# A Fourier filter with a maxout layer on one core: the first transform on bf16 loads without a fold, and another order for the exchanges

## The chip, the cores and the metric

The kernel runs on one core of a Trainium2 chip. TensorE (PE) multiplies matrices, VectorE (DVE) and ScalarE (ACT) move results out of PSUM and do elementwise work, GpSimd (POOL) does elementwise work and issues DMAs, SyncE (SP) issues DMAs. All DMAs of the core share its 16 DMA engines. The metric is the device time of one execution in microseconds, lower is better.

## What is computed

```python
def _attn_ref(x, filt_r, filt_i):            # x: 8 x 3072 x 256, filters: 1537 x 256
    X = np.fft.rfft(x, axis=1)
    F = (filt_r + 1j * filt_i)[None, :, :]
    Y = X * F
    return np.fft.irfft(Y, n=x.shape[1], axis=1).astype(np.float32)

def _moe_ref(x, w1, w2, w_out):              # x: 24576 x 256, w1, w2: 256 x 1024, w_out: 1024 x 256
    h1 = x @ w1
    h2 = x @ w2
    g = np.maximum(h1, h2)
    return (g @ w_out).astype(np.float32)
```

Each of the eight sequences is filtered in the frequency domain along its 3072 points, and each of the 24576 results goes through a layer with two sets of weights, of whose products the larger is taken. All inputs and the output are float32.

## The kernel before

**The transform.** 3072 points are 128 x 24. A batch of x is 128 partitions (p) by 24 columns (n) by 256 channels (d). S1 (`f1`, line 434) is a 128-point transform over p, one matmul for each two columns. Its result goes out to a DRAM buffer `ad` and comes back as `bt` in another arrangement (`f1_read`, 453): the 24 columns now lie on partitions, 48 rows in each half. Then `s2` (72) transforms over n into `px`, `product` (82) multiplies with the filter `F` on DVE, and `s3` (468) transforms back with the tables VP and VQ into `zt`. `zt` goes out to DRAM (`zd`) and comes back as `zr` (`z_read`, 460, three DMAs). `s4` (501) is the last 128-point transform, into `yt`: 512 tokens a tile, six tiles a batch. These two round trips through DRAM are the exchanges. A bt read moves 1.5 MB in four DMAs of runs of 512 bytes, a zr read 1.5 MB in three.

**The layer.** max(h1, h2) is h2 + max(h1 - h2, 0). `moe_h` (516) multiplies with Wd = w1 - w2, one of eight column blocks j at a time, into `ph`, and ACT or DVE takes max(., 0) into `gt`. `moe_o` (532) multiplies `gt` with Wo and `yt` with M = w2 Wo, and every tile ends in one `out` DMA of 512 KB, issued by POOL.

**S1 in the before kernel** works on folded input. `load_x` (419) brings fp32 rows with two DMAs of 512 KB, `fold` (427) on POOL makes sum and difference of two halves in bf16, and `f1` does four matmuls of 64 x 64 into two PSUM tiles, one of which ACT and one of which DVE evicts. Six `f1` a batch; every second one writes 512 KB to `ad`.

**Batch 0** goes without DRAM: `load_x0` (115) loads bf16 (POOL's DMA casts), `f1t` (254), `t1` (292), `s3t` (306) and `t2` (327) transpose on PE instead. Tables of sines come from ACT (`table_c`, 162, and lines 217 to 220 for U). The filter is loaded by POOL's DMAs in four pieces of rows (`load_f`, 125), each copied to the odd rows by SP (`double_f`, 136); its unused rows 48 to 63 are filled with zeros by DMAs from a small tile (`zero_f`, 140). The weights w1 and w2 share a buffer with `bt` and so are loaded late (line 378).

**The order.** The whole order is written out by hand. Tile tt of the layer has eight steps 8 tt + j; each step does `moe_h` of tile tt, `moe_o` of tile tt - 1, and then what the plan has put there; `s4` of the next tile follows at j = 4, or j = 6 where a new batch begins (its first tile is transformed in step 48 b - 2). `plan_batch` (560) takes, for a batch b, the steps of its loads, folds, `f1`, of the bt read, of the nine halves of the transform (s2 of one group and s3 of the group before), and of the zr read. Engines and queues take their work in this order, but each runs as far ahead as its own waits allow: SP's queue holds the ad writes, zd writes, bt and zr reads; POOL's holds the x loads, the folds and the outs. For batches from 4 on, with o = 48 (b - 2), the before plan has loads at o - 20, o - 8 and o, folds at o + 2, o + 6, o + 10, `f1` from o + 8 in steps of 3, the bt read at o + 28, s2 and s3 from o + 48 in steps of 4, and the zr read at o + 84. Batches 1 to 3 have lines of their own.

Of the kernel before, what the change touches and what calls it, by code (L numbers as in the profile page):

```python
# [21 lines left out]
TWO_PI = 6.283184  # L22
# [4 lines left out]
def kernel(  # L27
# [11 lines left out]
    nc = tc.nc  # L39
    V, S, G, TE = nc.vector, nc.scalar, nc.gpsimd, nc.tensor  # L40
# [4 lines left out]
    CF = const.tile([128, 128], BF16)  # L45
# [15 lines left out]
    xpool = ctx.enter_context(tc.tile_pool(name="xpool", bufs=3))  # L61
    sdpool = ctx.enter_context(tc.tile_pool(name="sdpool", bufs=2))
    apool = ctx.enter_context(tc.tile_pool(name="apool", bufs=2))
# [4 lines left out]
    bt = {}  # L68
# [36 lines left out]
    zf = tb.tile([16, 1024], BF16)  # L105
# [9 lines left out]
    def load_x0(c):  # L115
        if c % 3 == 0:
            xb["t"] = gpool.tile([128, 3, 4, D], BF16, tag="gt", name="xb")
        t_ = xb["t"][:, c % 3]
        G.dma_start(out=t_, in_=x[0].rearrange("(p n) d -> p n d", n=N2)[:, 4 * c:4 * c + 4, :])
        xb[c] = t_  # L120
# [15 lines left out]
    def double_f(s0, s1):  # L136
        for h in range(2):
            nc.sync.dma_start(out=F[64 * h + 1:64 * h + 48:2, :, s0:s1], in_=F[64 * h:64 * h + 48:2, :, s0:s1])

    def zero_f(s0, s1):  # L140
        for ri in range(2):
            n = (s1 - s0) // 4
            nc.sync.dma_start(out=F[48:64, ri, s0:s1].rearrange("p (k t) d -> p k (t d)", t=4),
                              in_=zf.rearrange("p (o d) -> p o d", o=1).to_broadcast([16, n, 1024]))
# [11 lines left out]
    uc = tb.tile([128, 2, 2, 64], FP32)  # L156
    rc = tb.tile([128, 2, 2, 64], FP32)
    col = tb.tile([128, 16], FP32)
    bb, mm, aa, n2, pp, pf, nn2 = (col[:, i:i + 1] for i in range(7))


    def table_c(k, p):
        V.tensor_scalar(uc[:, k, 0], row[:, 0:64], p, 0.25, OP.mult, OP.add)
        V.tensor_scalar(uc[:, k, 1], row[:, 0:64], p, None, OP.mult)
        V.tensor_scalar(uc[:, k, 1, 0:1], p, 64.0, 0.25, OP.mult, OP.add)
        wrap(uc[:, k], rc[:, k])
        if k == 0:
            S.activation(CE, uc[:, k].rearrange("p a x -> p (a x)"), AF.Sin, bias=zero, scale=TWO_PI)
        for r in range(2):
            S.activation((CF if k else C1)[:, 64 * r:64 * r + 64].rearrange("p (t a) -> p t a", a=2),  # L170
                         uc[:, k].rearrange("p a (t r) -> p r t a", r=2)[:, r], AF.Sin, bias=zero, scale=TWO_PI)
# [199 lines left out]
    for g in range(8):  # L371
        if g + 1 < 8:
            px[g + 1] = s2(0, g + 1, pxp, "px")
            products(g + 1)
        if g + 3 < 8:
            t1(g + 3, S)
        s3t(g, pq.pop(g), (S, S) if g < 7 else (S, V))
        if g == 4:
            wt = bpool.tile([128, 2, 2, HID], FP32, tag="bt", name="wt")
            w1f, w2f = wt[:, 0], wt[:, 1]  # L380
            for k in range(2):
                for w_, f_ in ((w2f, moe_w2), (w1f, moe_w1)):
                    nc.sync.dma_start(out=w_[:, :, 512 * k:512 * k + 512],
                                      in_=f_.rearrange("(c p) j -> p c j", p=128)[:, :, 512 * k:512 * k + 512])
# [28 lines left out]
    ad = {}  # L413
    zd = {}
    x2 = {}
    sd = {}
    at_ = {}

    def load_x(b, c):
        t_ = xpool.tile([128, 2, 4, D], FP32, tag="x2", name="x2")  # L420
        for h in range(2):
            src = bass.AP(x.tensor, x.offset + (b * N + 12 * h + 4 * c) * D,
                          [[N2 * D, 64], [64 * N2 * D, 2], [1, 4 * D]])
            G.dma_start(out=t_[64 * h:64 * h + 64].rearrange("p k n d -> p k (n d)"), in_=src)
        x2[b, c] = t_

    def fold(b, c):
        t_ = sdpool.tile([128, 2, 4, D], BF16, tag="sd", name="sd")
        x_ = x2.pop((b, c))
        G.tensor_tensor(t_[:, 0], x_[:, 0], x_[:, 1], OP.add)  # L430
        G.tensor_tensor(t_[:, 1], x_[:, 0], x_[:, 1], OP.subtract)  # L431
        sd[b, c] = t_

    def f1(b, n):
        c, u = divmod(n, 2)
        if n == 0:
# [4 lines left out]
        pa = [ps.tile([128, 2, D], FP32, tag="ps", name="pa") for _ in range(2)]
        for a in range(2):
            for h in range(2):
                TE.matmul(pa[h][64 * a:64 * a + 64], CF[64 * h:64 * h + 64, 64 * a:64 * a + 64],  # L444
                          sd[b, c][64 * h:64 * h + 64, a, 2 * u:2 * u + 2], start=True, stop=True,
                          skip_group_check=True)
        S.activation(at[:, 0, 2 * u:2 * u + 2], pa[0], AF.Copy)  # L447
        V.tensor_copy(at[:, 1, 2 * u:2 * u + 2], pa[1])  # L448
        if u == 1:
            nc.sync.dma_start(out=ad[b].rearrange("r (h n) d -> r h (n d)", h=2)[:, :, 4 * c * D:4 * c * D + 4 * D],  # L450
                              in_=at.rearrange("p h n d -> p h (n d)"))
# [186 lines left out]
```

## Time and profile before

| | before |
|---|---|
| median of 3 runs | 626.75 us (626.73 to 627.84) |
| the profiled execution, its own time | 625.69 us |
| its span, first to last instruction | 623.9 us |
| PE busy | 519.4 us (83%) |
| DVE, ACT, POOL busy | 323.2, 331.4, 186.5 us |
| mean granted TensorE clock | 0.913 |
| moved by DMA | 99.89 MB, 160 GB/s |
| x loads | 42 of 512 KB |
| first `ph` matmul (the layer begins) | 54.9 us |
| step 47, 95, 143, 191, 239 (first `gt` after a new batch's first tile) | 163.9, 237.7, 307.0, 376.4, 445.2 us |

Instructions are grouped by the line of the kernel; `out<-in` names tiles. "PE py L507 <- DMA zr<-zd: 41.7, 5, 11.1" says that PE's instruction of line 507 waited 41.7 us in total, five times, at most 11.1, for that DMA. In the chain of waits each row has a start, a length and what filled it. An `SPq` row in the timeline shows SP issuing DMAs; a DMA's data moves later.

### The profile page before, as it was taken

To read this page: it belongs to the slowest core of one execution; us is meant where nothing else is said; L and a number is where in the kernel's file an instruction comes from. 1 tells how busy PE (TensorE), PEld (TensorE's weight loads), DVE (VectorE), ACT (ScalarE), POOL (GpSimd) and SP (SyncE) were. 2 spreads that over 40 slices of the span, in tenths; PEclk is the share of its full clock that TensorE was granted. 3 is DMA by queue.
4 is the path that set the end of the run, shared out by engine and by line. 5 is a ranking of instruction groups with operands and counts; after the bars stand their busy time and mean duration, and the time that the engine had idled before them with its cause. 6 is when DMAs were issued, how large, how long until landed. Compare 5 with 4: busy or idle time off the path is not lost.

```text
span 623.9 us, 12287 instructions
## 1 busy us (share of the span) xinstructions
PE 519.4 (83%) x5094; PEld 349.0 (56%) x5172; DVE 323.2 (52%) x434; ACT 331.4 (53%) x587; POOL 186.5 (30%) x186
## 2 busy tenths in 40 slices
PE   5566580897699938999499959999699999999996
PEld 3344360564466625667366636667366666667774
DVE  6656330693158705773277515873277447733332
ACT  5462250465257624766266635765366656665551
POOL 6666851232343016411181017311370000000000
PEclk9856795799699988999799988999799999999999
DMA  7957799139976996469853994569844952351112
GB/s 124 147 129 174 172 257 147 51 95 255 275 104 202 195 178 203 138 173 201 239 156 101 232 253 134 153 166 233 227 128 134 174 208 81 99 187 76 59 45 101
DMA packets 73641, 99.89 MB, mean 160 GB/s; under 512 B 5809, under 2 KB 51378, under 8 KB 73586
## 3 DMA queue, kind: packets, MB, share of 16 engines
q1 hardware_dynamic: 55874, 48.25, 36.2%
q0 software_dynamic: 17712, 50.87, 30.7%
q8 instruction: 40, 0.66, 0.5%
q14 instruction: 15, 0.12, 0.1%
HBM read 53.48 MB, written 47.19 MB: 161 GB/s over the span
## 4 chain that ended last, share of the span: by engine, by line
PE 51%; DMA 21%; issue 17%; POOL 5%; DVE 2%; ACT 2%; SPq 1%; POOLq 0%; DVEq 0%; ACTq 0%
PE po L542 18%; PE ph L522 17%; DMA zr<-zd 6%; DMA zd<-zt 5%; PE pz L478 4%; PE po L545 4%; PE py L507 3%; DMA bt<-ad 3%; DMA F<-in_filt_r_dram 2%; PE pa L444 2%; PE px L78 2%; DMA ad<-at 2%; DVE pqt L85 2%; DMA xb<-in_x_dram 1%; DMA x<-in_x_dram 1%
## 5 line engine op out<-in xcount | busy, mean ns | idle before, releaser
L527 ACT ACTIVATE gt<-ph 128x512 bf16<-128x512 f32 x334 | 199.2, 597 | 134.7 <-PE ph L522 130.3
L542 PE MATMUL po<-Wo,gt 128*128 128x256 bf16 x1536 | 234.2, 276 | 4.4 <-issue 1.1
L522 PE MATMUL ph<-yt,Wd 128*128 128x512 bf16 x691 | 218.5, 389 | 4.0 <-DVE Wd L388 2.0
L542 PEld LDWEIGHTS <-gt 128*128 128x128 bf16 x1536 | 152.5, 99 | 102.5 <-issue 6.6
L85 DVE TENSOR_TENSOR pqt<-px,F 112x1024 bf16<-112x1024 f32 x124 | 146.0, 1219 | 80.0 <-PE px L78 71.7
L551 POOL DMA_DIRECT2D out_dram<-ot x48 | 26.8, 559 | 377.0 <-DVE ot L547 364.6
L547 DVE COPY ot<-po 128x512 f32<-128x512 f32 x96 | 66.1, 689 | 116.4 <-PE po L545 116.1
L522 PEld LDWEIGHTS <-Wd 128*128 128x128 bf16 x768 | 69.6, 100 | 27.8 <-issue 18.1
L482 ACT ACTIVATE zt<-pz 112x512 bf16<-112x512 f32 x112 | 60.7, 594 | 33.6 <-PE pz L478 32.0
L545 PE MATMUL po<-M,yt 128*128 128x256 bf16 x384 | 74.8, 277 | 0.0
L507 PE MATMUL py<-G,zr 128*128 128x128 bf16 x384 | 33.4, 234 | 43.2 <-DMA zr<-zd 41.7
L511 DVE TENSOR_SCALAR yt<-py 128x512 bf16<-128x512 f32 x48 | 32.9, 685 | 63.8 <-PE py L507 63.8
L509 ACT ACTIVATE yt<-py 128x512 bf16<-128x512 f32 x48 | 28.7, 599 | 67.5 <-PE py L507 67.4
L430 POOL TENSOR_TENSOR sd<-x 128x1024 bf16<-128x1024 f32 x21 | 49.4, 2353 | 37.3 <-issue 32.4
L507 PEld LDWEIGHTS <-zr 128*128 128x128 bf16 x384 | 25.9, 105 | 51.1 <-DMA zr<-zd 43.1
L431 POOL TENSOR_TENSOR sd<-x 128x1024 bf16<-128x1024 f32 x21 | 49.3, 2348 | 0.0
L78 PE MATMUL px<-bt,U 48*64 48x256 bf16 x512 | 27.9, 287 | 17.1 <-DMA bt<-ad 17.1
L545 PEld LDWEIGHTS <-yt 128*128 128x128 bf16 x384 | 38.2, 100 | 5.0
L525 DVE TENSOR_SCALAR gt<-ph 128x512 bf16<-128x512 f32 x50 | 34.1, 682 | 7.9 <-PE ph L522 7.8
L447 ACT ACTIVATE at<-pa 128x512 bf16<-128x512 f32 x42 | 25.1, 598 | 22.9 <-PE pa L444 22.5
L448 DVE CAST at<-pa 128x512 bf16<-128x512 f32 x42 | 28.6, 682 | 14.4 <-PE pa L444 11.0
L478 PE MATMUL pz<-pqt,VP 48*64 48x256 bf16 x448 | 30.7, 283 | 0.6 <-DVE pqt L85 0.2
(119 smaller groups left out, 280.1 us busy)
## 6 DMA issues: line engine op xcount, KB each, us to landing
out_dram<-ot POOLq DMA_DIRECT2D x48, 512.0 KB, 3.2
x<-in_x_dram POOLq DMA_DIRECT2D x42, 512.0 KB, 8.9
ad<-at SPq DMA_DIRECT2D x21, 512.0 KB, 4.2
bt<-ad SPq DMA_DIRECT2D x28, 384.0 KB, 13.0
zd<-zt SPq DMA_DIRECT2D x112, 96.0 KB, 3.0
zr<-zd SPq DMA_DIRECT2D x7, 768.0 KB, 8.4
zr<-zd SPq DMA_DIRECT2D x7, 512.0 KB, 6.6
wt<-in_moe_w_dram SPq DMA_DIRECT2D x4, 512.0 KB, 4.2
```

What stands on the lines that cost most here:

```text
L78: TE.matmul(px[r][64 * h:64 * h + 64, i], U[64 * r:64 * r + 48, 48 * t:48 * t + 64], bt[b][64 * r:64 * r + 48, t], start=True, stop=True, ...
L85: E.tensor_tensor(pqt, px[0:112].rearrange("p (o i) d -> p o i d", o=1).to_broadcast([112, 2, 2, D]), F[0:112, :, s0:s0 + 3:2], OP.mult)
L430: G.tensor_tensor(t_[:, 0], x_[:, 0], x_[:, 1], OP.add)
L431: G.tensor_tensor(t_[:, 1], x_[:, 0], x_[:, 1], OP.subtract)
L478: TE.matmul(pz[h][64 * r:64 * r + 64, i], W_[64 * h:64 * h + 48, c0_:c0_ + 64], pq[r][64 * h:64 * h + 48, ri, i], start=(ri == 0), stop=(r ...
L482: S.activation(zt[:, h, 2 * (g % 2):2 * (g % 2) + 2], pz[h][0:112], AF.Copy)
L507: TE.matmul(py[:, n], zr[b][:, 4 * i + n, 128 * dc:128 * dc + 128], G1, start=True, stop=True)
L522: TE.matmul(ph_, Wd[:, dc, 128 * j:128 * j + 128], y_[:, dc].rearrange("p a b -> p (a b)"), start=(dc == 0), stop=(dc == 1))
L527: S.activation(gt[tt][:, j], ph_, AF.Relu)
L542: TE.matmul(p_, g_[:, jj, 128 * n:128 * n + 128], Wo[:, jj], start=(jj == 0), stop=False)
L545: TE.matmul(p_, y_[:, dc, n], M[:, dc], start=False, stop=(dc == 1))
L547: V.tensor_copy(ot[tt][:, n - 1:n + 1], po[tt])
```

## The change

S1 takes the input as it is: `load_x` is one DMA that casts to bf16 (512 KB read, 256 KB written, all 128 partitions), `f1` is one matmul of 128 x 128 by 512 columns with the table C1 and one eviction, by ACT or DVE in turn, and every second of the now twelve `f1` a batch writes 256 KB to `ad`. The folds, their buffers and the table CF are gone. The plan has new steps for loads, `f1`, bt reads, transforms and zr reads. Batch 0's input comes in four pieces, of 8, 8, 4 and 4 columns. The filter comes in three pieces, and its zero rows are written by DVE, POOL and ACT, as part of a 32-row block that the loads then write into. U's sines come after three `f1t`, the table SW after those. The weights have a buffer of their own and are loaded behind the filter.

```diff
-    xpool = ctx.enter_context(tc.tile_pool(name="xpool", bufs=3))
-    sdpool = ctx.enter_context(tc.tile_pool(name="sdpool", bufs=2))
-    apool = ctx.enter_context(tc.tile_pool(name="apool", bufs=2))
+    xpool = ctx.enter_context(tc.tile_pool(name="xpool", bufs=8))
+    apool = ctx.enter_context(tc.tile_pool(name="apool", bufs=6))
+    wpool = ctx.enter_context(tc.tile_pool(name="wpool", bufs=1))
...
-    def load_x0(c):
-        if c % 3 == 0:
-            xb["t"] = gpool.tile([128, 3, 4, D], BF16, tag="gt", name="xb")
-        t_ = xb["t"][:, c % 3]
-        G.dma_start(out=t_, in_=x[0].rearrange("(p n) d -> p n d", n=N2)[:, 4 * c:4 * c + 4, :])
-        xb[c] = t_
+    for n0, n1 in ((0, 8), (8, 16), (16, 20), (20, 24)):
+        if n0 % 16 == 0:
+            xt = gpool.tile([128, 16, D], BF16, tag="gt", name="xt")
+        G.dma_start(out=xt[:, n0 % 16:n0 % 16 + n1 - n0], in_=x[0].rearrange("(p n) d -> p n d", n=N2)[:, n0:n1, :])
+        for n in range(n0, n1, 4):
+            xb[n // 4] = xt[:, n % 16:n % 16 + 4]
...
     def zero_f(s0, s1):
-        for ri in range(2):
-            n = (s1 - s0) // 4
-            nc.sync.dma_start(out=F[48:64, ri, s0:s1].rearrange("p (k t) d -> p k (t d)", t=4),
-                              in_=zf.rearrange("p (o d) -> p o d", o=1).to_broadcast([16, n, 1024]))
+        return F[32:64, :, s0:s1].rearrange("p c s d -> p c (s d)")
...
     V.memset(hpi, 1.570796)
+    V.memset(zero_f(0, 8), 0.0)
+    G.memset(zero_f(8, 20), 0.0)
+    for ri in range(2):
+        S.activation(F[32:64, ri, 20:32].rearrange("p s d -> p (s d)").bitcast(FP32), zero[32:64].to_broadcast([32, 1536]), AF.Copy)
...
-    S.activation(Uq[:, :, 0], v.rearrange("p t s j -> p t (s j)"), AF.Sin, bias=zero, scale=TWO_PI)
...
+    def table_u():
+        S.activation(Uq[:, :, 0], v.rearrange("p t s j -> p t (s j)"), AF.Sin, bias=zero, scale=TWO_PI)
+        S.activation(Uq[:, :, 1], rv.rearrange("p t s j -> p t (s j)"), AF.Sin, bias=hpi, scale=-TWO_PI)
...
-    for c in range(6):
-        load_x0(c)
-    load_f(0, 8)
-    double_f(0, 8)
-    zero_f(0, 8)
-    zero_f(8, 32)
-    for s0, s1 in ((8, 20), (20, 28), (28, 32)):
+    for s0, s1 in ((0, 8), (8, 20), (20, 32)):
         load_f(s0, s1)
         double_f(s0, s1)
+    wt = wpool.tile([128, 2, 2, HID], FP32, name="wt")
+    w1f, w2f = wt[:, 0], wt[:, 1]
+    for k in range(2):
+        for w_, f_ in ((w2f, moe_w2), (w1f, moe_w1)):
+            nc.sync.dma_start(out=w_[:, :, 512 * k:512 * k + 512],
+                              in_=f_.rearrange("(c p) j -> p c j", p=128)[:, :, 512 * k:512 * k + 512])
...
+    def load_x(b, c):
+        t_ = xpool.tile([128, 4, D], BF16, tag="xb", name="xb")
+        G.dma_start(out=t_, in_=x[b].rearrange("(p n) d -> p n d", n=N2)[:, 4 * c:4 * c + 4, :])
+        xb[b, c] = t_
...
-    for c in range(5):
+    for c in range(3):
         f1t(c)
+    table_u()
+    table_sw()
+    f1t(3)
+    f1t(4)
     tables_v(0)
     tables_v(1)
     f1t(5)
-    table_sw()
...
         if g == 6:
             G.dma_start(out=Wo, in_=moe_w_out.rearrange("(c p) j -> p c j", p=128))
+            for c in range(6):
+                load_x(1, c)
...
+    def f1(b, c):
+        if c == 0:
             ad[b] = dram.tile([128, N2, D], BF16, tag="ad", name="ad")
+        if c % 2 == 0:
+            at_[b] = apool.tile([128, 4, D], BF16, tag="at", name="at")
         at = at_[b]
...
+        pa = ps.tile([128, 2, D], FP32, tag="ps", name="pa")
+        TE.matmul(pa, C1, xb[b, c // 2][:, 2 * (c % 2):2 * (c % 2) + 2], start=True, stop=True)
+        if c % 2 == 0:
+            S.activation(at[:, 0:2], pa, AF.Copy)
+        else:
+            V.tensor_copy(at[:, 2:4], pa)
+            nc.sync.dma_start(out=ad[b][:, 2 * c - 2:2 * c + 2], in_=at)
...
-    for c in range(3):
-        load_x(1, c)
     plan(1, t2, 1, ps, "ps", (V,))
-    plan(2, prep_w2t)
     plan(3, t2, 2, ps, "ps", (V,))
-    plan(5, prep_m)
+    plan(5, prep_w2t)
     plan(6, t2, 3, ps, "ps", (V,))
+    plan(7, prep_m)
...
-    plan_batch(1, (), (0, 1, 2), ev(4, 1, 6), 12, ev(20, 2, 9), 38)
-    plan_batch(2, (8, 14, 20), (22, 25, 28), ev(30, 3, 6), 50, ev(62, 3, 9), 88)
-    plan_batch(3, (32, 42, 46), (48, 52, 56), ev(61, 3, 6), 81, ev(97, 4, 9), 132)
+    plan_batch(1, (), ev(2, 1, 12), 14, ev(24, 2, 9), 41)
+    plan_batch(2, ev(22, 2, 6), ev(30, 1, 12), 46, ev(57, 3, 9), 82)
+    plan_batch(3, ev(50, 2, 6), ev(58, 2, 12), 86, ev(98, 4, 9), 132)
     for b in range(4, B):
         o = 48 * (b - 2)
-        plan_batch(b, (o - 20, o - 8, o), (o + 2, o + 6, o + 10), ev(o + 8, 3, 6), o + 28, ev(o + 48, 4, 9), o + 84)
+        plan_batch(b, ev(o - 4, 4, 6), ev(o + 4, 2, 12), o + 37, ev(o + 46, 4, 9), o + 80)
```

In the new calls of `plan_batch` the arguments are the batch, the steps of the loads, of the `f1`, of the bt read, of the transform, and of the zr read; `ev(a, d, n)` is n steps from a on, d apart. `table_sw` keeps its six small DVE operations for SW and loses the table CF.

More of the change, by code (lines that the diff above doesn't have):

```diff
@@ L44 @@
     CE = const.tile([128, 128], BF16)
-    CF = const.tile([128, 128], BF16)
     G1 = const.tile([128, 128], BF16)
@@ L104 @@
     hpi = tb.tile([128, 1], FP32)
-    zf = tb.tile([16, 1024], BF16)
+    zf = tb.tile([16, 512], BF16)
     nyq = tb.tile([2, D], FP32)
@@ L154, in wrap @@
         V.tensor_tensor(u, u, r, OP.subtract)
-    uc = tb.tile([128, 2, 2, 64], FP32)
-    rc = tb.tile([128, 2, 2, 64], FP32)
+    uc = tb.tile([128, 2, 64], FP32)
+    rc = tb.tile([128, 2, 64], FP32)
     col = tb.tile([128, 16], FP32)
[L159 to L171, printed above, removed]
+    bb, mm, aa, n2, pp, nn2 = (col[:, i:i + 1] for i in range(6))
     V.memset(zero, 0.0)
@@ L176 @@
     V.memset(hpi, 1.570796)
+    V.memset(zero_f(0, 8), 0.0)
+    G.memset(zero_f(8, 20), 0.0)
+    for ri in range(2):
+        S.activation(F[32:64, ri, 20:32].rearrange("p s d -> p (s d)").bitcast(FP32), zero[32:64].to_broadcast([32, 1536]), AF.Copy)
     V.tensor_scalar(pp, pid, 1.0 / 128.0, None, OP.mult)
-    table_c(0, pp)
+    V.tensor_scalar(uc[:, 0], row[:, 0:64], pp, 0.25, OP.mult, OP.add)
+    V.tensor_scalar(uc[:, 1], row[:, 0:64], pp, None, OP.mult)
+    V.tensor_scalar(uc[:, 1, 0:1], pp, 64.0, 0.25, OP.mult, OP.add)
+    wrap(uc, rc)
+    S.activation(CE, uc.rearrange("p a x -> p (a x)"), AF.Sin, bias=zero, scale=TWO_PI)
+    for r in range(2):
+        S.activation(C1[:, 64 * r:64 * r + 64].rearrange("p (t a) -> p t a", a=2),
+                     uc.rearrange("p a (t r) -> p r t a", r=2)[:, r], AF.Sin, bias=zero, scale=TWO_PI)
     V.tensor_scalar(I128, row, pid, None, OP.is_equal)
@@ L216 @@
     wrap(nn2, t0_)
-    S.activation(Uq[:, :, 0], v.rearrange("p t s j -> p t (s j)"), AF.Sin, bias=zero, scale=TWO_PI)
     V.scalar_tensor_tensor(rv, v, -1.0, v, OP.mult, OP.max)
     V.tensor_scalar(rv[0:48, 0, 0, 0:1], nn2[0:48], -1.0, nn2[0:48], OP.mult, OP.max)
-    S.activation(Uq[:, :, 1], rv.rearrange("p t s j -> p t (s j)"), AF.Sin, bias=hpi, scale=-TWO_PI)
-    for s_, m_ in ((0, na), (1, aa)):
-        V.tensor_scalar(U[0:48, 24 * s_:24 * s_ + 24], U[0:48, 24 * s_:24 * s_ + 24], m_[0:48], None, OP.mult)
+    def table_u():
+        S.activation(Uq[:, :, 0], v.rearrange("p t s j -> p t (s j)"), AF.Sin, bias=zero, scale=TWO_PI)
+        S.activation(Uq[:, :, 1], rv.rearrange("p t s j -> p t (s j)"), AF.Sin, bias=hpi, scale=-TWO_PI)
+        for s_, m_ in ((0, na), (1, aa)):
+            V.tensor_scalar(U[0:48, 24 * s_:24 * s_ + 24], U[0:48, 24 * s_:24 * s_ + 24], m_[0:48], None, OP.mult)
     for t_ in (U, VP, VQ):
@@ L234, in table_sw @@
         V.tensor_scalar(SW, row, tgt, sgn, OP.is_equal, OP.mult)
-        V.tensor_scalar(pf, mm, 1.0 / 128.0, None, OP.mult)
-        table_c(1, pf)
     nc.sync.dma_start(out=nyq[1:2], in_=filt_r[1536:1537])
-    for c in range(6):
-        load_x0(c)
-    load_f(0, 8)
-    double_f(0, 8)
-    zero_f(0, 8)
-    zero_f(8, 32)
-    for s0, s1 in ((8, 20), (20, 28), (28, 32)):
+    for s0, s1 in ((0, 8), (8, 20), (20, 32)):
         load_f(s0, s1)
         double_f(s0, s1)
+    wt = wpool.tile([128, 2, 2, HID], FP32, name="wt")
[4 more added lines that the diff above has]
+                              in_=f_.rearrange("(c p) j -> p c j", p=128)[:, :, 512 * k:512 * k + 512])
+    ad = {}
+    zd = {}
+    at_ = {}
+    def load_x(b, c):
+        t_ = xpool.tile([128, 4, D], BF16, tag="xb", name="xb")
+        G.dma_start(out=t_, in_=x[b].rearrange("(p n) d -> p n d", n=N2)[:, 4 * c:4 * c + 4, :])
+        xb[b, c] = t_
     def spin(n):
@@ L377 @@
         s3t(g, pq.pop(g), (S, S) if g < 7 else (S, V))
[L378 to L384, printed above, removed]
         if g == 6:
             G.dma_start(out=Wo, in_=moe_w_out.rearrange("(c p) j -> p c j", p=128))
+            for c in range(6):
+                load_x(1, c)
     t2(0, ptp, "pt", (S, V))
@@ L411, in prep_m @@
         V.tensor_copy(M, pm)
[L413 to L436, printed above, removed]
+    def f1(b, c):
+        if c == 0:
             ad[b] = dram.tile([128, N2, D], BF16, tag="ad", name="ad")
-        if u == 0:
-            at_[b] = apool.tile([128, 2, 4, D], BF16, tag="at", name="at")
+        if c % 2 == 0:
+            at_[b] = apool.tile([128, 4, D], BF16, tag="at", name="at")
         at = at_[b]
[L441 to L451, printed above, removed]
+        pa = ps.tile([128, 2, D], FP32, tag="ps", name="pa")
[5 more added lines that the diff above has]
+            nc.sync.dma_start(out=ad[b][:, 2 * c - 2:2 * c + 2], in_=at)
     def f1_read(b):
@@ L558, in plan, with plan_batch @@
         todo.setdefault(step, []).append((fn, a))
-    def plan_batch(b, xs_, fs, s1s, read, s2s, zread):
+    def plan_batch(b, xs_, s1s, read, s2s, zread):
         for c, n in enumerate(xs_):
             plan(n, load_x, b, c)
-        for c, n in enumerate(fs):
-            plan(n, fold, b, c)
         for c, n in enumerate(s1s):
```

## The prediction

> **What bounds the kernel now.** I read the table of waits first, since PE's 519.4 us of busy time in a span of 623.9 leaves some 100 us to explain:
>
> ```profile
> PE py L507 <- DMA zr<-zd: 41.7, 5, 11.1
> PE px L78 <- DMA bt<-ad: 17.1, 3, 10.3
> PE pa L444 <- POOL sd L430: 6.1, 1, 6.1
> DVE pqt L85 <- DMA F<-in_filt_r_dram: 4.4, 1, 4.4
> DVE pqt L85 <- DMA F<-zf: 3.7, 1, 3.7
> ```
>
> PE waits for two exchanges through DRAM, `zr<-zd` before a batch's first tile and `bt<-ad` before its second transform, once for POOL's fold, and at the start DVE waits for the filter. Then the chain of waits where one batch follows another (steps 190 and 191; I date a step by its `gt<-ph` eviction, one per step):
>
> ```profile
> 360.11 6.61 DMA zd<-zt
> 366.86 7.52 DMA zr<-zd
> 374.43 1.03 PE py L507 x8
> ```
>
> The last zd write, three times its undisturbed 2.2 us, holds the zr read, and the zr read holds PE. The eight py matmuls after it take 1.03 us, 0.55 when warm: a stall is paid again in clock, about 1 us. What the DMA engines do meanwhile stands in busy time by stretches (columns: stretch, length, PE, PEld, DVE, ACT, POOL, PEclk, DMA share, GB/s):
>
> ```profile
> 3.00:12.40 9.40, 4.40 (x22) 2.17 (x21) 7.67 (x34) 3.62 (x7) 5.58 (x11) 1.00 1.05 182
> 60.00:70.00 10.00, 2.22 (x15) 0.88 (x14) 1.60 (x3) 0.62 (x2) 5.39 (x4) 0.77 1.04 217
> 98.00:108.00 10.00, 0.37 (x1) 0.00 (x0) 0.00 (x0) 0.00 (x0) 0.00 (x0) 0.50 1.27 126
> 168.60:180.80 12.20, 12.09 (x97) 8.80 (x97) 4.16 (x7) 7.16 (x12) 7.72 (x5) 1.00 1.23 146
> 367.00:374.40 7.40, 0.12 (x2) 0.00 (x0) 0.00 (x0) 0.20 (x1) 0.00 (x0) 0.65 1.05 269
> ```
>
> In all five the engines are full. Batch 0's bf16 loads (first row): six pieces of 512 KB read and 256 KB written, 1.57 MB at 171 to 182 GB/s, 1.4 us a piece. The fp32 x loads (second): 512 KB at 217 GB/s, 2.4 us each, 14.5 a batch. A bt read, 1.57 MB: 12.2 us of full engines (third and fourth). An out write, 512 KB, is 1.7 us (309 GB/s in the stretch 481.5 to 483.5). So x loads are what makes zd and zr slow. Last, the one chain that meets no x load and no bt read, batch 7's:
>
> ```profile
> 548.27 0.60 ACT L527 ACTIVATE gt<-ph 128x512 bf16<-128x512 f32 x1 [0.44 <-PE ph L522]
> 549.95 1.81 SPq L487 DMA_DIRECT2D zd<-zt  x4
> 554.44 1.29 SPq L463 DMA_DIRECT2D zr<-zd  x3
> ```
>
> From the step of the last s3 (320, at 548.3) to the zr issue: 6.2 us; about 1 us more to the first byte, 7.1 in all. The whole zr read, 1.57 MB at 293 to 311 GB/s, is 5 us; I use 4.7, as its first pieces go slowly beside little else.
>
> **S1.** 42 folds of 2.35 us leave POOL (98.7 us), worth what PE waited for them: 6.1 + 2.3, and the load in front, 9.5 us at steps 4 and 5 and 1 at step 9. Per batch, 24 matmuls (0.41 us for four) become 12 of 128 rows by 512 columns; the nearest row is ph, 0.43 us per two, so nothing in PE. Evictions stay 6 on ACT and 6 on DVE. Loads stay 6 issues of 0.6 us on POOL, but cost 8.4 us of DMA instead of 14.5. POOL and SP run ahead of the steps: a load goes out right behind the previous `out` in POOL's queue, whatever its planned step.
>
> **Startup.** Before, products(0) runs at 26.7, held by the zero rows, the next at 35.7, held by filter rows, and ph starts at 54.9. After: the zero rows cost DVE 1.8 us (2048 words, by the 0.91 us of the AT memset with 1024), ACT 2 x 1.45 (1536 elements, between 0.60 us for 512 and 1.02 for 1024), both while x arrives. POOL's memset of 6144 elements isn't in the trace: 2.4 us if it goes by words at the iotas' 0.76 ns (0.234 us for 128 elements, 0.137 for one), 9.2 if by elements at the w2b cast's 1.5 ns (1.53 us for 1024); I take 4.6, the words at the cast's rate. Behind it in POOL's queue wait all filter loads, but x's last piece lands at 12.5 anyway and they are behind it; at 9.2 us the cover is gone and some 4 us come back. 30 loads are issued where 40 were. So F's first piece is doubled at about 21, and U's Sin behind three f1t, which frees the AT evictions that waited until 11.9, has px there too: products(0) at 21.3. The second piece lands at about 27 by its share of the 26 us of nearly full DMA, less the zero rows' part. The six groups then take their 12.9 us (35.7 to 48.6) and 6.3 to the first ph: 46.2, I say **47** for 54.9 (45 to 51). Weights now come behind F on SP and are there by 40; DVE's 2.9 us of Wd stay on the path, so they win nothing more.
>
> **The exchanges.** Now batch 1: step 0 at 48; before took 19 us of work to step 13, where now the last f1 is, so 66 to 67. The ad write goes at 67.7 and lands at 70.7; bt's first byte 71.7, 12.2 us, plus x and out: x for step 22 goes after out of step 15, those for 24 to 30 after out of step 23 at 78; 2 + some 5 us share the engines. px at **91.5** (110.6 before). Step 40 is 29.6 later (28.0 from 110.6 to step 36, plus five f1 more), zr's first piece 9.2 after that: first tile of batch 1 at **130.5** (161.9). In step 41 the z_read stands ahead of f1 on SP, so batch 2's last ad write comes behind the zr read, and bt's first byte at 136: plus 12.2, out and three x loads (5.8): px of batch 2 at **153**, 9 after it is due. Before, this read was hidden.
>
> From here one pattern holds: on SP the bt read stands behind z_read, which waits for the last zd write. From the last s3's step to px: 7.1 + zr 4.7 + bt 12.2 + one out 1.7 + one x 1.4 + 0.6 for px = **27.7**. Due is px after 17.4 when 16 steps lie between (14.8 for steps 272 to 286, 2 more at 1.03, 0.5), 13.4 with the 12 steps of batch 4. PE's px is in front of s4, ACT and DVE starve with it, so a new stall of 10 us takes the place of the zr stall of 8 to 10, which goes (zr has 16 steps for 10 us). Batch 3: 35 us to step 81 (24 steps at 1.03, eight transforms at 0.8, f1), then 27.7 and one out and two x loads more (4.5): **220**. 32 steps with transform and f1 take 43.5 (308.4 to 351.9), so batch 4: 220 + 43.5 + 27.7 = **291.2**; 304.4 before. Batch 5 and 6: 71.2 each where 69.4 and 68.8 stood: 362.4, 433.6. Batch 7 has no x load: 69.8, px at 503.4; before, step 286 was reached with hardly a stall, at 506.2 by the same point. From there 117.7 + 1 for the clock: a span of 622.1, 1.8 below the 623.9 of before. The profiled execution of before took 625.7 with what lies around its span, so this one 623.9; the median of the runs shown, 626.75, is 1 above its profiled one, which gives 624.9, and I say **624.5**. So: 8 won at the start, 29 at batch 2's first px (182.4 before), 13 of them left at batch 4's, 3 at batch 7's.
>
> *Bounds of the chain:* if out and x queue behind bt, 24.6; if bt takes 13.5, as from 96.5 to 110, and the others 1 more, 30. It counts five times: -15 and +12. The zero rows: -2 and +4.
>
> The Trainium skill ("DMA: Bandwidth & Descriptors", Queues, rings and completion order) says that each DMA engine goes round the rings that have work, packet by packet. In the trace an out write lands after 2.9 us alone, and one that started behind a bt read (491.4) after 10.2, when that read was done, which fits turns no better than first come, first served. By the page's rule x and out come in between and the chain is 27.7; by plain order it is 24.6 and the time about 609.
>
> **Rivals.**
> - *The late bt read costs more (slower).* Place: px at step 46 of each batch; price: a chain of 29 to 30 us instead of 27.7, or POOL's memset at 9.2. From 28.4 on (five times 0.7 us over the forecast) the kernel is slower than 628; at 30 it is 636. For it: batch 7's 7 us are lost for sure, since its zr now comes with a bt read behind. Against: no x fp32 loads in the way.
> - *bt overlaps the zr read.* For it: small packets reach a share of 1.27 where large ones reach 1.05. Chain 24.6 to 25, time 609 to 611. Against: from 484.7 to 502.2 the parts (bt 12.2, two zd groups 3, out 1.7) add to 16.9 of 17.5 us.
> - *No change*, the two halves cancel: 625.5 to 628.
>
> Gains and losses are each near 30 us, so the sign is weakly held.
>
> **How the numbers follow.** Forecast, a small gain, 612 to 625.5: 0.37. bt overlaps, under 612: 0.14. No change, 625.5 to 628 (0.2%, about 1.25 us, is what a measurement can tell): 0.12. Slower: 0.37. Faster is the first two, 0.51. Chain bounds and memset give 608 to 638 and leave some 0.1 on each side; the forecast's own range is 615 to 631.
>
> **What would show it.** products(0) near 21 and ph near 47; no fold; waits of `py` for zr under 5 us in all and of `px` for bt near 65 to 70, in seven places, each behind a z_read on SP; x pieces landing 1.4 us apart. I am wrong if px waits little in the later batches, or if ph starts after 51.

## The result, and the profile after

The changed kernel takes 633.59 us (median of 11 executions, 629.99 to 637.25); the kernel before takes 626.73 us beside it (11 executions, 624.35 to 629.66). The ratio is 1.0111, with a 95% interval of 1.0078 to 1.0145: slower, by a good 1%. A ratio leaves out executions in the chip's slow state, which a median as given here does not; it matters for one run below, with two such executions of twelve. The profiled execution took 630.35 us, its span is 628.4 us, the mean granted clock 0.917 (0.913 before), POOL is busy for 85.7 us instead of 186.5, and the DMAs move 88.35 MB instead of 99.89.

First the table of waits of the changed kernel (line, releaser, us in total, times, longest):

```profile
PE px L77 <- DMA bt<-ad: 68.9, 20, 7.5
PE pa L264 <- ACT CE L171: 8.5, 1, 8.5
ACT F L164 <- POOL F L162: 3.9, 1, 3.9
PE py L485 <- DMA zr<-zd: 3.7, 1, 3.7
POOL F L131 <- ACT F L164: 2.7, 1, 2.7
```

The wait for zr, 41.7 us before, is 3.7; the wait for bt, 17.1 before, is 68.9. Together they grew by 14 us, and the wait for POOL's fold is gone. Three waits of the start are new. Where this stands in a batch is seen in batch 6, on SP's queue and then on PE (start, length, line, what, and in brackets the idle time before it with its releaser):

```profile
409.52 1.82 SPq L465 DMA_DIRECT2D zd<-zt  x4
414.70 1.84 SPq L441 DMA_DIRECT2D zr<-zd  x3
416.59 8.59 SPq L436 DMA_DIRECT2D bt<-ad  x4
```

```profile
427.88 0.29 PE L77 MATMUL px<-bt,U 48*64 48x256 bf16 x1 [2.83 <-DMA bt<-ad]
435.23 0.42 PE L77 MATMUL px<-bt,U 48*64 48x256 bf16 x2 [7.07 <-DMA bt<-ad]
437.01 0.58 PE L77 MATMUL px<-bt,U 48*64 48x256 bf16 x5 [1.36 <-DMA bt<-ad]
437.53 1.04 PE L485 MATMUL py<-G,zr 128*128 128x128 bf16 x8
```

The last zd write holds the zr read, the zr read stands ahead of the bt read in SP's order, and the first px matmuls need all four pieces of bt. They wait three times, 11.3 us in all, and the eight py matmuls behind them, whose zr has long been there, run at half clock (1.04 us; at full clock, at 479.9, 0.61). The busy time by stretches (stretch, length, PE, PEld, DVE, ACT, POOL, granted clock, DMA share, GB/s) has a full stretch while bt comes, an empty one just behind it, and, at 60 to 70 us, the place where the fp32 loads of x stood:

```profile
60.00:70.00 10.00, 9.90 (x87) 7.49 (x87) 6.31 (x10) 5.08 (x10) 0.00 (x0) 1.00 0.29 107
416.60:434.80 18.20, 8.69 (x62) 5.89 (x61) 2.08 (x3) 4.78 (x8) 1.07 (x2) 0.84 1.05 203
436.00:441.00 5.00, 3.77 (x21) 2.34 (x22) 3.43 (x4) 1.19 (x2) 0.00 (x0) 0.50 0.00 1
```

From 60 to 70 PE is busy for 9.90 us where it was 2.22. From 416.6 to 434.8 the engines are full, at 1.05, with the zr read, the bt read, one `out` and one load of x. From 436 to 441 they carry nothing, and PE has a clock of 0.50.

How the lead is won and lost shows in the times of single steps (the `gt` eviction of the step; the times of before stand in its table, step 287 was 507.1 and 383 was 613.6):

| step | after, us | ahead of before, us |
|---|---|---|
| first ph | 52.7 | 2.2 |
| 47 | 132.1 | 31.8 |
| 95 | 205.6 | 32.1 |
| 143 | 293.9 | 13.1 |
| 191 | 366.2 | 10.2 |
| 239 | 439.5 | 5.7 |
| 287 | 510.9 | -3.8 |
| 383 | 618.3 | -4.7 |

Between steps 95 and 143 the wait for bt shows as 14.0 us from the `gt` of step 98 to the next one, at 222.6. From step 143 on a batch takes 72.2, 73.3 and 71.5 us where it took 69.4, 68.8 and 61.9 before.

At the start (rows of POOL, ACT and DVE in order of engine):

```profile
3.73 5.21 POOL L162 MEMSET F<- 32x6144 bf16 x1
8.98 2.85 ACT L164 ACTIVATE F<-zero 32x1536 f32<-32x1536 f32 x2 [3.93 <-POOL F L162]
11.85 1.28 ACT L171 ACT_TABLE_LOAD   x1
13.14 0.40 ACT L171 ACTIVATE CE<-uc,zero 128x128 bf16<-128x128 f32 x1
3.98 5.02 DVE L167 TENSOR_SCALAR uc<-row,col 128x64 f32<-128x64 f32 x1
4.15 4.88 DVE L168 TENSOR_SCALAR uc<-row,col 128x64 f32<-128x64 f32 x1
26.66 4.62 DVE L84 TENSOR_TENSOR pqt<-px,F 112x1024 bf16<-112x1024 f32 x4 [0.41 <-DMA F<-in_filt_r_dram]
33.70 4.76 DVE L84 TENSOR_TENSOR pqt<-px,F 112x1024 bf16<-112x1024 f32 x4 [2.42 <-DMA F<-F]
```

ACT's zero rows write the same tile as POOL's memset and wait for it, and ACT's first table CE waits behind them: it is made at 13.1, and PE is idle for 8.5 us until then. Two DVE instructions that took 0.26 and 0.25 us before last 5.02 and 4.88 us beside the memset and end with it. They make `uc`, the input of CE, which is therefore finished at 9.8 only: without ACT's rows CE would have come some 3 us sooner at most. The filter's first load goes out at 8.9, the others from 12.1 on. The first products run at 26.7, as before, and the second piece of the filter, copied to its odd rows, releases the next ones at 33.7, two us earlier than before.

### The profile page after: what moved, and what is told of

It is laid out like the page before. It is cut to its first block, busy times and chain, and to the rows that moved or that the text cites. A ratio compares the mean times of both kernels' runs of the same rounds, so it can differ in the third digit from the quotient of the medians.

```text
span 628.4 us, 12103 instructions
## 1 busy us (share of the span) xinstructions
PE 522.6 (83%) x5007; PEld 354.7 (56%) x5088; DVE 324.7 (52%) x429; ACT 333.8 (53%) x588; POOL 85.7 (14%) x135
## 2 busy tenths in 40 slices
DMA packets 73057, 88.35 MB, mean 141 GB/s; under 512 B 5881, under 2 KB 51450, under 8 KB 73002
## 4 chain that ended last, share of the span: by engine, by line
issue 73%; PE 10%; POOL 9%; DMA 5%; ACT 2%; DVE 1%; SPq 0%; POOLq 0%; DVEq 0%
POOL out_dram L529 3%; PE ph L500 3%; POOL xb L252 2%; DMA bt<-ad 2%; PE po L520 2%; DMA F<-F 1%; PE pa L424 1%; POOL F L133 1%; POOL F L162 1%; PE pz L456 1%; POOL F L128 1%; DMA F<-in_filt_r_dram 1%; PE py L485 1%; PE pt L340 1%; PE po L523 0%
## 5 line engine op out<-in xcount | busy, mean ns | idle before, releaser
L84 DVE TENSOR_TENSOR pqt<-px,F 112x1024 bf16<-112x1024 f32 x124 | 146.1, 1220 | 154.0 <-PE px L77 151.0
L77 PE MATMUL px<-bt,U 48*64 48x256 bf16 x512 | 32.6, 293 | 68.9 <-DMA bt<-ad 68.9
L500 PEld LDWEIGHTS <-Wd 128*128 128x128 bf16 x768 | 73.3, 101 | 24.6 <-issue 8.0
L77 PEld LDWEIGHTS <-U 48*64 48x64 bf16 x512 | 15.1, 110 | 76.0 <-DMA bt<-ad 55.9
L485 PE MATMUL py<-G,zr 128*128 128x128 bf16 x384 | 32.0, 230 | 4.0 <-DMA zr<-zd 3.7
L424 PE MATMUL pa<-xb,C 128*128 128x512 bf16 x84 | 32.7, 389 | 0.0
```

The source lines that it names most:

```text
L77: TE.matmul(px[r][64 * h:64 * h + 64, i], U[64 * r:64 * r + 48, 48 * t:48 * t + 64], bt[b][64 * r:64 * r + 48, t], start=True, stop=True, ...
L84: E.tensor_tensor(pqt, px[0:112].rearrange("p (o i) d -> p o i d", o=1).to_broadcast([112, 2, 2, D]), F[0:112, :, s0:s0 + 3:2], OP.mult)
L424: TE.matmul(pa, C1, xb[b, c // 2][:, 2 * (c % 2):2 * (c % 2) + 2], start=True, stop=True)
L485: TE.matmul(py[:, n], zr[b][:, 4 * i + n, 128 * dc:128 * dc + 128], G1, start=True, stop=True)
L500: TE.matmul(ph_, Wd[:, dc, 128 * j:128 * j + 128], y_[:, dc].rearrange("p a b -> p (a b)"), start=(dc == 0), stop=(dc == 1))
```

## Experiments

The changed kernel is the base of a run unless another is named. Ratios are to the kernel before on the same chip.

**Reading bt earlier.** The f1 results that bt needs are written long before its read is planned. The first run gives the bt reads of batches 3 to 7 the places they had in the kernel before:

```diff
-    plan_batch(3, ev(50, 2, 6), ev(58, 2, 12), 86, ev(98, 4, 9), 132)
+    plan_batch(3, ev(50, 2, 6), ev(58, 2, 12), 81, ev(98, 4, 9), 132)
-        plan_batch(b, ev(o - 4, 4, 6), ev(o + 4, 2, 12), o + 37, ev(o + 46, 4, 9), o + 80)
+        plan_batch(b, ev(o - 4, 4, 6), ev(o + 4, 2, 12), o + 28, ev(o + 46, 4, 9), o + 80)
```

> The changed kernel (633.6 us) with the bt reads of batch 3 and of batches 4 to 7 planned earlier (step 81 for 86, o + 28 for o + 37), so that on SP they stand before the z_read of the batch in front and run during its last steps. Theory A (the place of the bt read on SP, behind z_read, makes the new wait): the px waits of batches 3 to 7, some 11 us beyond the step each, go; the zr read, now behind the bt read, gives back 1 to 4 us a batch; time 585 to 605. Rival B (the DMA engines can't move more, so the wait only changes its name, as in the kernel before where zr waits 8 to 10 us): zr waits of 8 to 10 us a batch come instead, time 618 to 632.

601.28 us, ratio 0.9631 (0.958 to 0.9682). Its waits:

```profile
PE py L485 <- DMA zr<-zd: 26.9, 6, 6.5
PE px L77 <- DMA bt<-ad: 14.8, 4, 5.9
```

The wait for bt falls from 68.9 to 14.8, all of it in batches 1 and 2, whose reads were left where they are; px of batches 3 to 7 no longer waits at all. Part of the gain, 23 us, comes back as a wait for zr. That the gain depends on the order on SP and not on the long lead is what the second run tells: its bt reads go out just ahead of the zr read (batch 3 at step 81, batch 4 at 131, later ones at o + 31).

> The changed kernel with only the order of the two reads turned round on SP: bt read planned at step 81 (batch 3), 131 (batch 4), o + 31 (batches 5 to 7), just ahead of the z_read, whose step stays. Same bytes in nearly the same stretch. Theory A: the bt read starts some 4 to 6 us sooner, doesn't wait for the last zd write to land, and ends when px is due or 1 to 3 us later; zr comes after it and is 0 to 4 us late for s4; time 595 to 612, not as good as the earlier read. Rival B: the sum of both waits stays, 625 to 634.

607.82 us, ratio 0.9713 (0.9676 to 0.9749). Its waits:

```profile
PE px L77 <- DMA bt<-ad: 31.9, 13, 5.7
PE py L485 <- DMA zr<-zd: 19.4, 5, 8.1
```

By the ratios the first run is 30 us below the changed kernel and this one 25, so most of it comes from changing places with the zr read alone. Both runs end in the range of the theory that the place behind the zr read is what costs.

**The three parts of the change.** The changed kernel with the old plan; each of the old steps for a load or an `f1` now has two (the lines that these replace are left out):

```diff
+    tw = lambda steps: [n for n in steps for _ in range(2)]
+    plan_batch(1, (), tw(ev(4, 1, 6)), 12, ev(20, 2, 9), 38)
+    plan_batch(2, tw((8, 14, 20)), tw(ev(30, 3, 6)), 50, ev(62, 3, 9), 88)
+    plan_batch(3, tw((32, 42, 46)), tw(ev(61, 3, 6)), 81, ev(97, 4, 9), 132)
+        plan_batch(b, tw((o - 20, o - 8, o)), tw(ev(o + 8, 3, 6)), o + 28, ev(o + 48, 4, 9), o + 84)
```

> The changed kernel (bf16 loads, unfolded S1, its startup) with the steps of the kernel before for loads, f1 (two of the twelve at each of the six steps), bt reads, transforms and zr reads. Theory A (the plan costs, S1 on bf16 loads gains): zr waits as in the kernel before, but x loads of 8.4 us a batch instead of 14.5 leave 3 to 6 us of the 8 to 10; px no longer waits in the later batches; time 595 to 612, below both kernels. Rival C (bf16 loads with a cast are no lighter for the engines when they run beside other transfers): zr waits stay at 8 to 10, time 620 to 628.

587.66 us, ratio 0.939 (0.9362 to 0.9417), better than either theory said. The kernel before with S1 alone (casting loads, unfolded `f1`, the old start and this same doubled plan):

```diff
-        for h in range(2):
-            src = bass.AP(x.tensor, x.offset + (b * N + 12 * h + 4 * c) * D,
-                          [[N2 * D, 64], [64 * N2 * D, 2], [1, 4 * D]])
-            G.dma_start(out=t_[64 * h:64 * h + 64].rearrange("p k n d -> p k (n d)"), in_=src)
+        G.dma_start(out=t_, in_=x[b].rearrange("(p n) d -> p n d", n=N2)[:, 4 * c:4 * c + 4, :])
...
-        G.tensor_tensor(t_[:, 0], x_[:, 0], x_[:, 1], OP.add)
-        G.tensor_tensor(t_[:, 1], x_[:, 0], x_[:, 1], OP.subtract)
...
+        TE.matmul(pa, C1, xb[b, c // 2][:, 2 * (c % 2):2 * (c % 2) + 2], start=True, stop=True)
```

> The kernel before with S1 alone changed: bf16 loads, one matmul an f1, two f1 at each of the six old steps, no folds; its startup and its plan of steps as they were. Theory A (the lighter loads are what gains in e3_old_plan, 587.7 us; the new startup brings 2 us at most): 588 to 594. Rival E (the startup's changes carry a good part of the gain): 600 to 615.

595.23 us, ratio 0.9498 (0.9462 to 0.9534): S1 is worth 31 us. It misses the first theory's range by a us. The distance to the run before, 0.0108 of 627 us or 7 us, is what the rest of the change (start, filter in three pieces, the weights' own buffer) is worth with that plan; the intervals of the two don't meet. And the kernel before, with its folds and fp32 loads, under the new exchange steps (its three loads and folds and six `f1` a batch spread over the places that the new ones have; the old lines are left out):

```diff
+    plan_batch(1, (), (0, 1, 2), ev(3, 2, 6), 14, ev(24, 2, 9), 41)
+    plan_batch(2, (20, 22, 26), (28, 32, 36), ev(31, 2, 6), 46, ev(57, 3, 9), 82)
+    plan_batch(3, (50, 52, 56), (58, 64, 70), ev(60, 4, 6), 86, ev(98, 4, 9), 132)
+        plan_batch(b, (o - 4, o, o + 8), (o + 4, o + 10, o + 18), ev(o + 6, 4, 6), o + 37, ev(o + 46, 4, 9), o + 80)
```

> The kernel before, folds and fp32 loads kept, with the changed kernel's steps for the bt reads, the transforms and the zr reads, and the nearest steps for loads, folds and its six f1. Theory A (the plan costs by itself, wherever it is put): zr waits go, px waits of 10 to 17 us come in each batch and fp32 loads of 2.4 us stand in their way; time 640 to 680. Rival F (the late bt read hurts only because bf16 loads run closer behind): 620 to 632.

686.57 us, ratio 1.095 (1.0915 to 1.0985), above the range of both theories. Its waits:

```profile
PE px L78 <- DMA bt<-ad: 109.9, 21, 10.9
PE py L507 <- DMA zr<-zd: 2.4, 1, 2.4
```

It has the same exchange of waits as the changed kernel, from zr to bt, with more to pay. In part the fp32 loads now share the engines with the bt read: in batch 5 two of them land at 411.5 and 414.6, just ahead of bt's third piece at 415.2; batches 3 to 6 wait 12.8 to 17.8 us for bt (9.9 to 13.0 in the changed kernel), and batch 7, beside which no x is loaded, 9.7 (8.5). How much of the difference this is was not measured by itself. The parts thus stand, by the ratios and taken in this order: S1 wins 31 us, the start and the weights 7, and the new plan costs 1.0111 less 0.939 of 627 us, 45. Together that is the 7 us by which the changed kernel is slower. Taken in the other order the plan costs 60 us on the kernel before, and S1 with the new start wins 53 under the new plan (1.095 less 1.0111): the parts depend on each other.

**The start.** The zero rows written later and by words: ACT's behind its first tables, POOL's, as fp32, between the loads of the first and second filter piece.

```diff
-    G.memset(zero_f(8, 20), 0.0)
-    for ri in range(2):
-        S.activation(F[32:64, ri, 20:32].rearrange("p s d -> p (s d)").bitcast(FP32), zero[32:64].to_broadcast([32, 1536]), AF.Copy)
...
     S.activation(CE, uc.rearrange("p a x -> p (a x)"), AF.Sin, bias=zero, scale=TWO_PI)
...
+    for ri in range(2):
+        S.activation(F[32:64, ri, 20:32].rearrange("p s d -> p (s d)").bitcast(FP32), zero[32:64].to_broadcast([32, 1536]), AF.Copy)
...
     for s0, s1 in ((0, 8), (8, 20), (20, 32)):
+        if s0 == 8:
+            for ri in range(2):
+                G.memset(F[32:64, ri, 8:20].rearrange("p s d -> p (s d)").bitcast(FP32), 0.0)
```

> The changed kernel with the zero rows written so that nothing waits for POOL's memset: ACT's after the tables C1 and CE, POOL's two memsets by words and behind the first piece of the filter. Theory D (POOL's memset of 5.2 us holds ACT's zero rows, through them CE and the filter loads, and makes two DVE operations of 0.26 us take 5 us): first ph at 46 to 49 for 52.7, time 4 to 6 us less, 627 to 630. Rival: the filter's DMAs set the start anyway and the wait of batch 1 for bt takes the rest: ph at 51 to 53, time 632 to 634.

633.34 us, ratio 1.0131 (1.0075 to 1.0187): no difference from the changed kernel. CE is made at 5.2 us, but the memset now waits for the copy of the first piece and holds the loads of the second:

```profile
19.54 2.83 POOL L238 MEMSET F<- 32x1536 f32 x2 [5.18 <-DMA F<-F]
```

First ph comes at 56.6, 4 us later, instead of earlier as expected. In the profiled execution that delay is still there at step 191 (371.8 for 366.2) and less at the end of the span (631.3 for 628.4). The run tells of its own mistake more than of the theory. A better start: ACT writes rows 20 to 32 behind its tables, DVE the others in words, POOL none.

```diff
-    V.memset(zero_f(0, 8), 0.0)
-    G.memset(zero_f(8, 20), 0.0)
-    for ri in range(2):
-        S.activation(F[32:64, ri, 20:32].rearrange("p s d -> p (s d)").bitcast(FP32), zero[32:64].to_broadcast([32, 1536]), AF.Copy)
...
+    for ri in range(2):
+        S.activation(F[32:64, ri, 20:32].rearrange("p s d -> p (s d)").bitcast(FP32), zero[32:64].to_broadcast([32, 1536]), AF.Copy)
+    for ri in range(2):
+        V.memset(F[32:64, ri, 0:8].rearrange("p s d -> p (s d)"), 0.0)
...
+    for ri in range(2):
+        V.memset(F[32:64, ri, 8:20].rearrange("p s d -> p (s d)"), 0.0)
     def table_u():
```

> The changed kernel with other zero rows at the start: rows of piece 20 to 32 by ACT behind its first tables, the rest by DVE in fp32 words, nothing by POOL; plan untouched. First ph at 47 to 50 for 52.7. Theory A, the missed start was a term of the sum that lasts to the end: px of batch 1 and all later steps come 3 to 5 us earlier, 628 to 631. Rival B, the start is swallowed by the first bt wait, as the forecast's 91.5 for batch 1's px was met in spite of a late ph: px of batch 1 at 90 to 91.5 and 632 to 635.

632.06 us, ratio 1.0094 (1.0059 to 1.0128), an interval that shares most of its length with that of the changed kernel. The first products run at 23.9, three us earlier, and wait again:

```profile
23.93 4.62 DVE L84 TENSOR_TENSOR pqt<-px,F 112x1024 bf16<-112x1024 f32 x4 [0.75 <-PE px L77]
32.49 3.49 DVE L84 TENSOR_TENSOR pqt<-px,F 112x1024 bf16<-112x1024 f32 x3 [3.94 <-DMA F<-F]
```

So once the zero rows are out of the way the filter's second piece sets the start: it comes at 32.5 for 33.7, first ph at 51.6 for 52.7, which misses the expected 47 to 50. px of batch 1 follows at 90.6 for 91.2, px of batch 2 comes later (155.8 for 153.9) and the span is the same 628.4. With a gain of one us the run can't tell whether a start of 47 would have lasted to the end.

**The clock behind a stall.** PE is kept at work in the seven long waits, with matmuls into a PSUM tile that nobody reads, ahead of the first, second and fourth px matmul of a batch:

```diff
+                    if i == 0 and any(fill) and (h, r) != (1, 0):
+                        for _ in range(fill[r + h]):
+                            TE.matmul(pd, Wd[:, 0, 0:128], Wo[:, 0:2].rearrange("p a d -> p (a d)"),
+                                      start=True, stop=True, skip_group_check=True)
...
-                px = s2(b, g, ps, "ps")
+                px = s2(b, g, ps, "ps", ((5, 14, 3) if b == 1 else (8, 24, 4)) if g == 0 else (0, 0, 0))
```

> The changed kernel with TensorE kept at work in its seven long waits for bt: before the first px matmul of a batch, before the second and before the fourth stand 8, 24 and 4 matmuls of 128x128 by 512 columns (5, 14, 3 in batch 1) whose result is read by nobody; at 0.215 us each at full clock that is 7.7 us of a wait of 8.5 to 13. Theory A, the clock after a stall is worth about 1 us as forecast: seven times 1 us, 625 to 629. Theory B, the half clock behind a stall costs 2.3 us each time, the 4.4 us from px to the next step less 2.1 of work: 616 to 621. Rival C, what follows the stall is the refilling of the pipe (px to product to s4 to ph), not clock, or the extra matmuls delay px: 632 to 640, with py at full clock behind the stall all the same.

The median is 629.16 us, the ratio 1.0005 (0.9974 to 1.0037), whose interval lies below that of the changed kernel: 0.0106 of 627 us, 6.6 us for seven stalls, 0.9 each. Over all twelve executions the ratio of the means is 1.0028, which makes it 5.2 us, 0.7 each. Batch 7, on PE, in the changed kernel:

```profile
507.42 0.42 PE L77 MATMUL px<-bt,U 48*64 48x256 bf16 x2 [5.43 <-DMA bt<-ad]
508.47 0.58 PE L77 MATMUL px<-bt,U 48*64 48x256 bf16 x5 [0.63 <-DMA bt<-ad]
508.99 1.04 PE L485 MATMUL py<-G,zr 128*128 128x128 bf16 x8
516.01 0.30 PE L456 MATMUL pz<-pqt,VP 48*64 48x256 bf16 x4
```

and with the filled waits:

```profile
500.35 5.35 PE L81 MATMUL pd<-Wo,Wd 128*128 128x512 bf16 x24
507.38 0.38 PE L83 MATMUL px<-bt,U 48*64 48x256 bf16 x5 [0.48 <-DMA bt<-ad]
507.69 0.62 PE L491 MATMUL py<-G,zr 128*128 128x128 bf16 x8
513.55 0.30 PE L462 MATMUL pz<-pqt,VP 48*64 48x256 bf16 x4
```

From the last px to the first pz are 7.54 us in the one and 6.17 in the other: 1.4 us are clock. The rest of the delay behind a stall, until the next `gt` comes, is there with a warm PE too (3.8 us from the last px to the `gt` of step 288, 4.4 before): it is the way through product, py, yt and ph. The theory of 2.3 us a stall falls, that of 1 us holds by its reason (its range ended at 629). In batches 4, 5 and 6 the last px matmuls waited 0.13 us or less for data when the added ones were done, so these came too long there, in batch 4 by some 3 us (its second px matmul runs 8.4 us after the first, 5.3 without them), and the gain is rather a lower bound.

**A better version.** The start of the change, with `f1` in batches from 4 on done by step o + 21, bt read at o + 24, and the zr read one step earlier (three in batches 1 and 3, none in batch 2); the old lines are left out:

```diff
+    plan_batch(1, (), tw(ev(4, 1, 6)), 12, ev(20, 2, 9), 38)
+    plan_batch(2, tw((14, 16, 20)), ev(26, 1, 12), 40, ev(57, 3, 9), 82)
+    plan_batch(3, tw((48, 50, 52)), ev(58, 2, 12), 81, ev(96, 4, 9), 129)
+        plan_batch(b, tw((o, o + 2, o + 8)), tw(ev(o + 6, 3, 6)), o + 24, ev(o + 46, 4, 9), o + 79)
```

> The changed kernel with each exchange started as soon as its data can be there: f1 of batch 2 ends before the z_read of batch 1 (steps 26 to 37, bt read at 40), bt reads at 81, then o + 24, in front of the z_read of the batch ahead; x loads from o on; transforms from o + 46, z_read at o + 79. Theory A: px waits only in batch 1 (5 to 9 us), zr waits of 0 to 3 us a batch, time 548 to 568. Rival B (DMA engines are the bound): some 5 us a batch stay, 575 to 590.

572.44 us, ratio 0.9112 (0.907 to 0.9154), between the two ranges. From step 96 on no step takes over 5 us; three stalls are left, of 9.3 us at step 20, 14.2 at 57 and 10.0 at 94, all before batch 3's transform. The theory had the first of them in its sum, with 5 to 9 us; the second it had taken as gone, and the third, a wait for zr, it had put at 0 to 3. The same with all zero rows on DVE in words, the late ones ahead of U's table:

> e7_reads_early_all with all zero rows written by DVE, by words and block by block, the first behind the tables, the others behind the table of U's angles, so that no POOL memset is left and ACT makes CE first. Theory D (POOL's memset cost the start some 5 us and a start is worth its full length where no exchange waits): first ph at 47 to 50 for 52.7, time 2 to 5 us below e7. Rival: the 7 us on DVE are paid in the tables, ph at 52 to 55, no gain.

571.14 us, ratio 0.9094 (0.9062 to 0.9126); first ph at 50.5 for 53.1, half a microsecond past the expected range. The 1.3 us between the medians are less than what the intervals separate. The start with ACT's and DVE's zero rows, under this plan:

> The plan with all reads early, with the same start as the run before. Beside the 571 of the plan with all zero rows on DVE, where these rows held U's table and SW: first ph 1 to 3 us before its 50.5, and 568 to 571; rival, the weights' arrival sets ph, which stays at 50 to 51, and 570 to 573.

571.5 us, ratio 0.9129 (0.9099 to 0.9158); first ph at 50.3, within the ranges of the rival, whose reason (the arrival of the weights) was not tested. These three can't be told apart. All beat both kernels, by some 56 us the one before and by 62 the changed one.

## Why the prediction was wrong

**What held.** The mechanism was there as forecast: the zr wait goes (3.7 us, under 5 forecast), a px wait takes its place in seven places (68.9 us, 65 to 70 forecast). Six of them stand behind a zr read on SP; the forecast said all seven, but batch 1's read (step 14) has no zr read ahead of it, and its px waits 6.3 us all the same. The folds left POOL, which gives back 100.8 us, and PE's busy time grew by 3.2 us only. The loads of x land 1.2 us apart, at 93.4, 94.7, 95.9 and 97.1 (1.4 forecast). The times of px, forecast and measured:

| batch | 1 | 2 | 3 | 4 | 5 | 6 | 7 | end of span |
|---|---|---|---|---|---|---|---|---|
| forecast | 91.5 | 153 | 220 | 291.2 | 362.4 | 433.6 | 503.4 | 622.1 |
| measured | 91.2 | 153.9 | 221.0 | 291.5 | 363.7 | 437.0 | 508.5 | 628.4 |

In the working, 136 + 12.2 + 5.8 for batch 2's px is 154.0 and not the 153 that it writes, so it was nearer still. The chain from the last s3's step to px, put at 27.7 us (26.3 in batch 7), measures 27.2, 27.9, 29.2 and 26.5 in batches 4 to 7. With `out` and x behind bt it would have been 24.6, which no batch shows, and in batch 6 an `out` issued at 419.2, after bt's third piece (417.6), landed at 430.3, before that piece (435.2). The Trainium skill ("DMA: Bandwidth & Descriptors", Queues, rings and completion order), by which each DMA engine goes round the rings that have work, fits this.

**What failed** is the sum of small terms under two large ones of opposite sign: 32 us won until step 95, and 37 lost until the end. The forecast was 624.5, the median is 633.6. The 9.1 us between them are these:

- *The clock behind a stall, 4.0 us.* This is the step that failed most. The working names it, "about 1 us" a stall, and counts it once, behind batch 7's px. The 43.5 us for 32 steps come from a stretch of before that starts without a stall; from a late px to the last s3's step it takes 44.32, 44.04 and 44.93 (2.8 us more in three batches), and from batch 7's px to the end 119.95 for 118.7. In the run with filled waits the same stretches take 43.67, 43.67, 43.89 and 118.56: some 3.4 of the 4.0 us are gone, so they were clock. Only the last of them is unsteady: the run with a better start, which fills nothing, has 118.7 there.
- *The chain, 2.0 us:* 0.22, 1.53 and 0.23 in batches 5 to 7. With the 0.3 us by which batch 4's px came late this makes the 6.3 us of the span. Batch 6's 29.2 differs from one execution to the next: the runs with late zero rows, with filled waits and with a better start, whose plan is the same, have 27.6, 28.0 and 28.5 there. What makes the difference stays open.
- *The median over the profiled execution, 2.2 us.* The working puts it at 1 us, as before; it is 3.2 here. Executions of the changed kernel spread over 7.3 us, those of before over 5.3, and the profiled one was among the fastest. The other 0.6 us is rounding and what lies around the span.

The start failed too, but not in the end's time. 8 us were to be won, with the first products at 21.3 and ph at 47; 2.2 were, with products at 26.7 and ph at 52.7, and the text had named a ph after 51 as a sign of error. POOL's memset took 5.21 us where 4.6 was taken, within its bounds. What was wrong was the cover: "they are behind it" counted only the loads queued behind the memset on POOL. ACT's rows go into the same tile and stand ahead of CE, and DVE was shut out meanwhile, and no step asked for either. And the second filter piece, put at 27, came at 33.7, and at 32.5 without any memset on POOL. That px of batch 1 was met all the same is the work of a second error: from the eviction of step 13 to px are 18.7 us, where the working has 24.5, since it let four x loads share the engines that land only after px (93.4 to 97.1).

Of the rivals, the slower one came true in its sign, but not by its price: its own point was a chain above 28.4, and three of four batches are below that. The memset at 9.2 did not come. "bt overlaps the zr read" is refuted by the chains. "No change", at most 628, is missed by 5.6 us. A forecast that adds +30 and -30, from terms good to one us each and repeated from batch to batch, could not hold the sign, and the prediction called it weakly held itself.

## What to carry to other kernels

When a read is moved in a queue, ask what stands ahead of it there: a bt read that could have gone nine steps earlier waited behind a zr read that waits for the newest data, and changing places gave 25 of the 30 us that the earlier read gave. A cost that follows each stall belongs in the period, multiplied by the stalls, and not once at the end. Where one edit makes the traffic lighter and another moves the waits, time each alone: here they were worth -38 and +45 us (-53 and +60 in the other order), and the total of +7 tells nothing of either.

## What the runs showed of the hardware

- A memset on POOL of 6144 bf16 elements on 32 partitions took 5.21 us, 0.85 ns an element; the same rows as fp32 words, two memsets of 1536 elements, took 2.83 us, 0.92 ns a word. So words nearly halve it.
- Two DVE instructions with fp32 in and out, of 0.26 and 0.25 us in the kernel before, lasted until that memset ended (5.02 and 4.88 us). The Trainium skill ("SBUF — State Buffer", SBUF: two separate sides) says that GpSimd and a DVE instruction in a two-port mode share a pair of ports, which the first one holds for its whole instruction. The two rows agree with that; that they ran in such a mode no run here shows.
- ACT's copy as its first instruction cost a second load of tables: 1.28 us at 3.8 and again at 11.9, ahead of the first sine. In the two runs with another start, where the sines come first, there is one load, at 0.7.
- With the waits filled, the clock fell behind a stall in which PE was idle for no more than 2.07 us at a time (batch 6; last row of the two below, against the 0.50 of the same stretch above). The Trainium skill ("TensorE: Matmul & The Clock Gate", What's actually happening) gives an idle window of about 3.4 us for that; here shorter gaps were enough.

```profile
404.00:436.00 32.00, 29.93 (x236) 18.81 (x234) 9.49 (x13) 13.78 (x24) 2.00 (x4) 1.00 0.80 183
436.00:441.00 5.00, 4.87 (x28) 2.72 (x29) 3.13 (x4) 1.19 (x2) 0.00 (x0) 0.66 0.02 4
```
